# The subtraction of the state softmax's maximum moves from Pool to VectorE, right behind the transposes of the scores

## The chip, the core and the metric

The kernel runs on one core of a Trainium2 chip. The metric is the time of one execution on the device, in microseconds (us). The core has five engines that run side by side, each through its own instructions in order: PE (TensorE, matmuls and transposes; weight loads are listed apart as PEld), DVE (VectorE), ACT (ScalarE), POOL (GpSimd) and SP (SyncE, which issues the DMAs). An instruction that depends on another engine's result waits on a semaphore, and everything behind it on its own engine waits too.

## The reference

Three stages follow each other. The first is a two-way attention between 512 tokens and 32 state rows per head, for 8 batches (b) of 8 heads with 64 columns each:

```python
scores = scale * np.matmul(x, state.transpose(0, 1, 3, 2))      # tokens x states
a = softmax(scores, axis=-1)                                    # over the 32 states
xread = np.matmul(a, state)
scores2 = scale * np.matmul(state, x.transpose(0, 1, 3, 2))     # states x tokens
scores2 = scores2 - scores2.max(-1, keepdims=True)              # over the 512 tokens
a2 = np.exp(scores2)
a2 /= a2.sum(-1, keepdims=True) + 1e-09
sread = np.matmul(a2, x)
```

The second is a soft mixture of experts over all 4608 rows (512 tokens and 32 state rows per batch) with 8 experts of 4 slots; the third is a gated unit, `(silu(x @ w_gate) * (x @ w_val)) @ w_out`, on the same rows. Everything is in float32, and the result is compared with the reference in float32.

## The kernel before

**Stages.** The attention loop handles one batch per turn, b = 0 to 6, and then batch 7 in a tail of its own that works in halves. After it come the slots of the mixture (up to about 106 us), the two groups of experts, whose weights stream in while they run (up to about 145 us), and a main loop of 17 blocks of rows times 6 pieces of the gated unit (from about 152 us to the end). The order of the instructions on every engine is the order of the calls in the source: it is written out by hand.

**One turn of the attention loop.** `scores(b)` multiplies the states by the tokens on PE (L241): rows are 4 heads x 32 states, two groups q = 0, 1, columns are 512 tokens. ACT copies the product with the scale into the buffer `stsA` (L250, named atA in the profile; there is one such buffer, used by all batches). `scores_max(b)` takes the negated maximum over the 512 tokens on DVE (L255, tile nm). These scores serve both softmaxes:

- `attn_sub(b)` transposes the *unshifted* scores on PE in 8 pieces (the helper `tr8`, L267), so that tokens become rows, and DVE takes the maximum over the 32 states and subtracts it, in two halves (L277, L278, L277, L278). `attn_exp` takes the exponential of each half on ACT (L284), `attn_norm` sums on DVE and multiplies by the reciprocal on POOL (L291 to L295).
- `state_shift(b)` adds the negated maximum over the tokens to the scores in place, once per group q. It can only begin when the transposes of `attn_sub` have read the unshifted scores. `state_tr(b)` then transposes the shifted scores, also with `tr8` (L267, so one line has both transposes), and ACT takes the exponential of the whole (L311, tile e). The product with the tokens follows in the next turn (`sread_mm`, L321), and its division on DVE (L330 to L337).

Between these lie pieces of the batches b-1 and b-2: the transposes of the normalized weights (L344) and the products for the mixture's logits and slots (L354, L375, L382, L389, with ACT copies at L346, L363, L380 and L393). `load_T` (L233, L234) transposes the tokens of a later batch on PE, and ACT copies them. At b = 0 the projection of the states on the router stands in addition (L1005, with an ACT copy L1007).

**What sets the order around the change.** In the loop PE has: scores, transposes of a later batch, `sread_mm(b-1)`, logits of b-2, `attn_sub`'s 8 transposes, `attn_tr(b-1)`, `slots_mm(b-2)`, `state_tr`'s 8 transposes, `logits_mm(b-1)`. ACT has: the copy of the scores (L250), the copies of later tokens (L234), `logits_exp(b-2)`, two small copies, the two exponentials of `attn_exp` (L284), the exponential of `state_tr` (L311), two small copies (L363, L393), and the next turn's L250. The large PSUM tiles come from `pbig`, three buffers in turn, so the scores of the next turn take the buffer that `attn_sub`'s DVE instructions have read.

**The tail.** For batch 7 the maximum over tokens and `state_shift` follow both halves of L1030 and L1031 on DVE; then come `logits_tr(5)` (DVE copy L382), `slots_mm(5)` on PE between two rows of filler matmuls (L305), the halves' normalization (L1047 to L1052, one half of it on POOL), and `state_tr(7)`.

**The loads.** One SP queue issues all loads in order (L156) into a ring of 17 buffers; a load waits until its buffer is released by the matmuls that read it, or, for some expert weights, until an attention buffer is free (`free(...)`).

Of the kernel before, what the change touches and what calls it, by code (L numbers as in the profile page):

```python
# [12 lines left out]
ALU = mybir.AluOpType  # L13
# [47 lines left out]
def bc(ap, n):  # L61
    shape = list(ap.shape)
    return ap.rearrange("p (a o) -> p a o", o=1).to_broadcast([shape[0], shape[1], n])
# [3 lines left out]
def attn_moe_glu_kernel(  # L67
# [14 lines left out]
    pe, act, dve, pool = nc.tensor, nc.scalar, nc.vector, nc.gpsimd  # L82
# [43 lines left out]
    def pbig(shape, dt=F32):  # L126
        bcnt[0] += 1
        return psum(bcnt[0] % 3, shape, dt)
# [115 lines left out]
    def scores(b):  # L244
        x_ = xT.pop(b) if b in XT_PE else got.pop(("xt", b))
        p = pbig([128, 2, S])
        score_mm(b, x_, p, slice(0, S))
        done()
        t = stsA
        act.activation(out=t, in_=p, func=AF.Copy, scale=SCALE)  # L250
        sts[b] = t

    def scores_max(b):
        nm = sm.tile([128, 2], F32, tag="nm2", name="nm2")
        dve.tensor_reduce(out=nm, in_=sts[b], axis=AX.X, op=ALU.max, negate=True)  # L255
        RZ[b] = nm

    def state_shift(b):
        nm, t = RZ.pop(b), sts[b]
        for q in range(2):  # L260
            pool.tensor_scalar(out=t[:, q, :], in0=t[:, q, :], scalar1=nm[:, q:q + 1], scalar2=None, op0=ALU.add)  # L261

    def tr8(src):
        p = pbig([128, 4, 256])
        for j in range(4):
            for q in range(2):
                pe.transpose(p[:, j, q * 128:(q + 1) * 128], src[q][:, j * 128:(j + 1) * 128], ident)  # L267
        return p

    def attn_sub(b):  # L270
        t = sts[b]
        v = tr8([t[:, 0, :], t[:, 1, :]])
        a = wk.tile([128, 4, 256], F32, tag=f"a{b % 3}", name="a")
        for i in range(2):
            vi, ai = (u[:, 2 * i:2 * i + 2, :].rearrange("p j (h s) -> p (j h) s", s=NS) for u in (v, a))
            m1 = sm.tile([128, 16], F32, tag="m1", name="m1")
            dve.tensor_reduce(out=m1, in_=vi, axis=AX.X, op=ALU.max)  # L277
            dve.tensor_tensor(out=ai, in0=vi, in1=bc(m1, NS), op=ALU.subtract)  # L278
        A[b] = a

    def attn_exp(b):
        a = A[b]
        for i in range(2):
            act.activation(out=a[:, 2 * i:2 * i + 2, :], in_=a[:, 2 * i:2 * i + 2, :], func=AF.Exp)  # L284
# [12 lines left out]
    def heat(n, i=None, src=None):  # L297
        src = ident if src is None else src
        p = pbig([128, 128]) if i is None else psum(i, [128, 128])
        for _ in range(n):  # L300
            pe.matmul(out=p, lhsT=src, rhs=src, start=True, stop=True)
# [5 lines left out]
    def state_tr(b):  # L307
        t = sts[b]
        p = tr8([t[:, 0, :], t[:, 1, :]])
        e = wk.tile([128, 4, 256], F32, tag="e2", name="e2")  # L310
        act.activation(out=e, in_=p, func=AF.Exp)  # L311
        E2N[b] = e

    def sread_mm(b):
        x_, e = got.pop(("xn", b)), E2N.pop(b)
        p = psmall([128, 130])
        for q in range(2):
            for j in range(4):
                for c in range(4):
                    k = 128 * q + 32 * c  # L320
                    pe.matmul(out=p[32 * c:32 * c + 32, 65 * q:65 * q + 65], lhsT=e[:, j, k:k + 32],  # L321
                              rhs=x_[:, j, c, 65 * q:65 * q + 65],
                              start=(j == 0), stop=(j == 3))
        done()
        P4[b] = p

    def sread_out(b):
        p = P4.pop(b)
        z = sm.tile([128, 2], F32, tag="z2", name="z2")
        dve.tensor_scalar(out=z, in0=p[:, 0:130:129], scalar1=EPS, scalar2=None, op0=ALU.add)  # L330
        r2 = sm.tile([128, 2], F32, tag="r2", name="r2")
        dve.reciprocal(out=r2, in_=z)
        o = 32 * (b % 4)
        for c in range(4):
            dst = srC[o:o + 32, b // 4, 2 * c:2 * c + 2, :]
            cc = slice(32 * c, 32 * c + 32)
            dve.tensor_tensor(out=dst, in0=p[cc, 1:129].rearrange("p (q d) -> p q d", q=2), in1=bc(r2, D)[cc], op=ALU.mult)  # L337

    def attn_tr(b):
        a = A[b]  # L340
        p = pbig([128, 2, S])
        for j in range(4):
            for q in range(2):
                pe.transpose(p[:, q, j * 128:(j + 1) * 128], a[:, j, q * 128:(q + 1) * 128], ident)  # L344
        t = wk.tile([128, 2, S], F32, tag="at", bufs=1, name="at")
        act.copy(out=t, in_=p)  # L346
        AT[b] = t

    def logits_mm(b):
        t = AT.pop(b)  # L350
        p = psmall([128, 128])
        for q in range(2):
            for j in range(4):
                pe.matmul(  # L354
                    out=p[32 * j:32 * j + 32, :], lhsT=SP[:, b, q, :], rhs=t[:, q, j * 128:(j + 1) * 128],
                    start=(q == 0), stop=(q == 1),
                )
        P6[b] = p
# [8 lines left out]
    def logits_exp(b, n=128):  # L367
        t = LE[b]
        act.activation(out=t[:n, 1, :], in_=t[:n, 0, :], func=AF.Exp, bias=md[:n, b:b + 1], accum_out=ds[:n, b:b + 1])

    def logits_tr(b):
        t = LE.pop(b)
        p = psmall([128, 2, 128])
        for i in range(2):
            pe.transpose(p[:, i, :], t[:, i, :], ident)  # L375
        e = wk.tile([128, 128], F32, tag="edn", bufs=2, name="edn")
        lg = Lg[:, 2 + 4 * b:6 + 4 * b, :]
        for f in (1, 0) if b == B - 3 else (0, 1):
            if f:
                act.copy(out=lg, in_=p[:, 0, :].rearrange("p (j s) -> p j s", s=NSL))  # L380
            else:
                dve.tensor_copy(out=e, in_=p[:, 1, :])  # L382
        EdN[b] = e

    def slots_mm(b, alloc=psmall):
        e, a = EdN.pop(b), A.pop(b)
        p = alloc([128, 256])
        for j in range(4):
            pe.matmul(out=p[32 * j:32 * j + 32, :], lhsT=e[:, 32 * j:32 * j + 32], rhs=a[:, j, :], start=True, stop=True)  # L389
        P4["q"] = p  # L390
# [4 lines left out]
    def build_stB(g):  # L395
        p = psum(g, [128, 4, 128])
        for pr in range(4):
            pe.transpose(p[:, pr, :], stN[:, g, 2 * pr:2 * pr + 2, :].rearrange("p h d -> p (h d)"), ident)
        dve.tensor_copy(out=stB[:, 4 * g:4 * g + 4, :, :], in_=p.rearrange("p r (b s) -> p b r s", s=NS))
# [550 lines left out]
    with tc.manual_schedule():  # L950
# [16 lines left out]
        def ok(b):  # L967
            return 0 <= b < B

        def at(b, k):  # L970
            for half in range(2):
                if k in (LT[half], 99):
                    load_T(b + 1, half)

        at(-1, 99)
        for b in range(B - 1):
            scores(b)
            at(b, 0)
            if ok(b - 2):
                logits_exp(b - 2)  # L980
            scores_max(b)
            if b == 0:
                heat(HB)
                build_stB(1)
            if ok(b - 1):
                sread_mm(b - 1)
                sread_out(b - 1)
            if ok(b - 2):
                logits_tr(b - 2)
            attn_sub(b)  # L990
            state_shift(b)
            if ok(b - 1):
                attn_tr(b - 1)
            attn_exp(b)
            if ok(b - 2):
                slots_mm(b - 2)
            state_tr(b)
            attn_norm(b)
            if b == 0:
                p = pbig([128, 2, 512])  # L1000
                for bb in range(B):
                    for pr in range(4):
                        for hh in range(2):
                            r = slice(64 * hh, 64 * hh + 64)
                            pe.matmul(out=p[32 * pr:32 * pr + 32, hh, 32 * bb:32 * bb + 32], lhsT=stB[r, bb, pr, :],  # L1005
                                      rhs=phs[r, pr, :], start=True, stop=True)
                act.copy(out=SP.rearrange("p b q s -> p q b s"), in_=p[:, :, 0:256].rearrange("p q (b s) -> p q b s", s=NSL))  # L1007
            if ok(b - 1):
                logits_mm(b - 1)
                logits_max(b - 1)  # L1010
            if ok(b - 2):
                slots_out(b - 2)
            if b == 5:
                sr_T(0)
            if b == 6:
                sr_mm(0)

        b = B - 1
        x_ = xT.pop(b) if b in XT_PE else got.pop(("xt", b))
        t = stsA  # L1020
# [374 lines left out]
```

## Time and profile before

| quantity | value |
|---|---|
| median of 3 runs | 490.19 us (488.57, 490.19, 491.98) |
| profiled execution | 489.67 us, of which 487.6 us from the first to the last instruction |
| mean granted TensorE clock | 0.993 of full speed |
| PE busy | 452.9 us (93%) |
| DVE busy | 314.4 us (64%) |
| ACT busy | 254.7 us (52%) |
| POOL busy | 181.9 us (37%), of which L261 24.9 us in 16 instructions |
| moved by DMA | 74.36 MB |

The span is the stretch from the first to the last instruction of the profiled execution; the run's own time has 2.07 us around it. Busy time counts only instructions that compute. In the timeline, a row gives the start, the length, the engine, the line of the source, the operation, the tiles out<-in with their shapes, how many instructions were merged, and in square brackets the idle time of the engine just before, with what ended it. Ends of matmuls are modelled, and the records of neighbouring instructions of one engine can overlap by about a tenth of a microsecond.

### The profile page before, as it was taken

Reading aid. Unit: us, or ns where it says so; the run is one execution under the profiler, and the core shown is the slowest. Engines: PE = TensorE matmul, PEld = TensorE weight load, DVE = VectorE, ACT = ScalarE, POOL = GpSimd, SP = SyncE. Lnnn points to the kernel's source line nnn. Section 1 sums busy time; section 2 is a strip of 40 time slices with the busy share of each in tenths; the row PEclk is TensorE's granted clock in tenths of the full one; section 3 lists DMA queues with packets and bytes.
Section 4 is the critical chain, followed back from the end, with each engine's and each line's share of the span. In section 5 each row is a group of like instructions: output and inputs, shape, how many; then the busy total and the mean of one; then the engine's idle time right before and its main releaser. Section 6 shows DMA issues by size and latency. Waiting matters only on the chain.

```text
span 487.6 us, 9247 instructions
## 1 busy us (share of the span) xinstructions
PE 452.9 (93%) x3661; PEld 248.5 (51%) x3661; DVE 314.4 (64%) x627; ACT 254.7 (52%) x432; POOL 181.9 (37%) x150
## 2 busy tenths in 40 slices
PE   7788888899898998998999899899999999999996
PEld 5555566654445454454455354455555555555553
DVE  3577767856928966868989879876433344344454
ACT  1366776433616988777456365545444444444441
POOL 1354444308203433343343243342433333333331
PEclk9799999999999999999999999999999999999999
DMA  8999992869999940102000000000011112112124
GB/s 310 425 417 414 416 382 66 309 228 379 419 400 422 417 171 2 57 30 86 2 1 1 0 1 0 1 1 3 0 44 43 44 43 69 61 46 76 54 86 172
DMA packets 16218, 74.36 MB, mean 152 GB/s; under 512 B 1584, under 2 KB 2992, under 8 KB 9392
## 3 DMA queue, kind: packets, MB, share of 16 engines
q1 hardware_dynamic: 16176, 73.78, 38.6%
q8 instruction: 28, 0.46, 0.4%
q14 instruction: 14, 0.11, 0.1%
HBM read 64.87 MB, written 8.91 MB: 151 GB/s over the span
## 4 chain that ended last, share of the span: by engine, by line
PE 75%; DVE 9%; DMA 4%; issue 4%; POOL 3%; ACT 3%; SPq 0%; ACTq 0%; DVEq 0%; POOLq 0%
PE p L1279 49%; PE p L1245 8%; DMA u<-in_wo_dram 3%; POOL atA L261 3%; PE p L267 3%; PE p L241 2%; PE p L481 2%; PE p L512 1%; DVE sh L1250 1%; DVE gvf L567 1%; PE s L321 1%; PE s L732 1%; PE p L233 1%; DMA u<-in_xt_dram 1%; PE s L744 1%
## 5 line engine op out<-in xcount | busy, mean ns | idle before, releaser
L1279 PE MATMUL p<-wo,hl 128*128 128x512 f16 x1020 | 235.1, 379 | 4.4 <-DVE osb L1290 3.3
L1259 POOL TENSOR_TENSOR hl<-sh,hl 128x512 f16<-128x512 f32 x102 | 125.9, 1235 | 202.3 <-ACT hl L1258 111.6
L1279 PEld LDWEIGHTS <-hl 128*128 128x128 f16 x1224 | 119.1, 98 | 130.0 <-issue 4.7
L1250 DVE SCALAR_TENSOR_TENSOR sh<-p,segk,sh 128x512 f32<-128x512 f32 x102 | 76.4, 749 | 93.8 <-ACT sh L1246 85.7
L1258 ACT CAST hl<-sh 128x512 f16<-128x512 f32 x102 | 62.9, 617 | 115.9 <-PE p L1279 80.9
L1246 ACT ACTIVATE sh<-p,sg 128x512 f32<-128x512 f32 x85 | 58.4, 686 | 5.7 <-PE p L1245 1.0
L1290 DVE SCALAR_TENSOR_TENSOR osb<-p,segm,osb 128x512 f32<-128x512 f32 x62 | 45.3, 746 | 10.9 <-PE p L1279 10.9
L1279 PE MATMUL p<-bqm,hl 128*128 128x512 f16 x204 | 46.8, 379 | 0.0
L1245 PE MATMUL p<-cstack,gvs 128*128 128x256 f16 x272 | 41.2, 273 | 2.7 <-DVE gvs L778 1.4
L261 POOL TENSOR_SCALAR atA<-atA,nm 128x512 f32<-128x512 f32 x16 | 24.9, 1566 | 38.3 <-PE p L267 23.3
L1245 PEld LDWEIGHTS <-gvs 128*128 128x128 f16 x272 | 25.9, 98 | 20.9 <-issue 3.2
L267 PE MATMUL p<-cs,atA 128*128 128x128 f32 x120 | 19.4, 298 | 12.5 <-POOL atA L261 10.8
L267 PEld LDWEIGHTS p<-cs,atA 128*128 128x128 f32 x120 | 14.6, 150 | 17.0 <-POOL atA L261 16.9
L1245 PE MATMUL p<-cstack,gv 128*128 128x256 f16 x136 | 20.6, 273 | 0.9 <-DVE segm L805 0.9
L255 DVE TENSOR_REDUCE nm<-atA 128x2 f32<-128x1024 f32 x8 | 9.7, 1219 | 14.3 <-ACT atA L250 14.3
L1288 ACT ACTIVATE osb<-p,segk 128x512 f32<-128x512 f32 x26 | 17.1, 687 | 3.3 <-PE p L1279 3.1
L567 DVE SCALAR_TENSOR_TENSOR gvf<-u,gvf 128x512 uint32<-128x512 uint32 (+1 forms) x22 | 18.6, 860 | 0.1
L295 POOL TENSOR_TENSOR a<-a,r 128x1024 f32<-128x1024 f32 x7 | 13.4, 1916 | 13.8 <-DVE r L294 13.8
L571 DVE SCALAR_TENSOR_TENSOR gvf<-u,gvf 128x512 uint32<-128x512 uint32 (+1 forms) x22 | 18.1, 846 | 0.1
L1245 PEld LDWEIGHTS <-gv 128*128 128x128 f16 x136 | 13.0, 98 | 10.1 <-issue 1.7
L512 PE MATMUL p<-u,exq 128*32 128x256 f32 x256 | 14.8, 381 | 1.5 <-DMA u<-in_w_dram 0.8
L561 ACT ACTIVATE gvf<-u 128x512 f32<-128x512 f32 (+1 forms) x22 | 15.3, 715 | 0.0
(254 smaller groups left out, 502.6 us busy)
## 6 DMA issues: line engine op xcount, KB each, us to landing
u<-in_w_dram SPq DMA_DIRECT2D x24, 1024.0 KB, 14.2
u<-in_wgv_dram SPq DMA_DIRECT2D x12, 1024.0 KB, 16.3
u<-in_xn_dram SPq DMA_DIRECT2D x8, 1040.0 KB, 18.1
out_dram<-osb SPq DMA_DIRECT2D x15, 512.0 KB, 2.8
early<-in_w_dram SPq DMA_DIRECT2D x12, 512.0 KB, 8.7
u<-in_wo_dram SPq DMA_DIRECT2D x5, 1024.0 KB, 13.9
u<-in_xt_dram SPq DMA_DIRECT2D x3, 1024.0 KB, 7.6
u<-in_wo_dram SPq DMA_DIRECT2D x2, 512.0 KB, 10.2
```

The costliest lines, as they stand in the source:

```text
L261: pool.tensor_scalar(out=t[:, q, :], in0=t[:, q, :], scalar1=nm[:, q:q + 1], scalar2=None, op0=ALU.add)
L267: pe.transpose(p[:, j, q * 128:(q + 1) * 128], src[q][:, j * 128:(j + 1) * 128], ident)
L512: pe.matmul(out=SO[g][i][32 * j:32 * j + 32, :], lhsT=hT[g, k // 4][:, k % 4, 32 * j:32 * j + 32], rhs=u[:, j, :], start=(k == 0), stop=(k ...
L567: dve.scalar_tensor_tensor(out=tu[:, c], in0=lo[:, c], scalar=29, in1=tu[:, c], op0=ALU.logical_shift_right, op1=ALU.bitwise_or)
L571: dve.scalar_tensor_tensor(out=tu[:, c], in0=hi[:, c], scalar=0x80000000, in1=tu[:, c], op0=ALU.bitwise_and, op1=ALU.bitwise_or)
L1245: pe.matmul(out=p[v][:, 256 * i:256 * i + 256], lhsT=GV[2 * q + i][v], rhs=rhs, start=True, stop=True)
L1246: act.activation(out=sh[:, 0, :], in_=p[0], func=AF.Silu, scale=sgs[q])
L1250: dve.scalar_tensor_tensor(out=sh[:, 1, :], in0=p[1], scalar=(kap0[0] if k == 0 else seg_scale(*seg)[0][q]), in1=sh[:, 0, :], op0=ALU.mult ...
L1258: act.copy(out=t[:, 0, :], in_=sh[:, 1, :])
L1259: pool.tensor_tensor(out=t[:, 1, :], in0=sh[:, 1, :], in1=t[:, 0, :], op=ALU.subtract)
L1279: pe.matmul(out=accs[i], lhsT=t[:, u // 2, c], rhs=WO[2 * q + j][:, u % 2, :], start=first and u == 0 and j == 0, stop=last and (j, u) == ...
L1290: dve.scalar_tensor_tensor(out=o, in0=a, scalar=rsc, in1=o, op0=ALU.mult, op1=ALU.add)
```

## The change

Both calls of `state_shift` now issue their two instructions on DVE instead of POOL. In the loop the call also moves: from behind `attn_sub(b)` into it, directly behind the 8 transposes, and so ahead of the DVE maxima and subtractions of the other softmax. In the tail the call stays where it was (behind `scores_max`), on the other engine. Nothing else changes; no DMA is issued by these lines.

```diff
     def state_shift(b):
         nm, t = RZ.pop(b), sts[b]
         for q in range(2):
-            pool.tensor_scalar(out=t[:, q, :], in0=t[:, q, :], scalar1=nm[:, q:q + 1], scalar2=None, op0=ALU.add)
+            dve.tensor_scalar(out=t[:, q, :], in0=t[:, q, :], scalar1=nm[:, q:q + 1], scalar2=None, op0=ALU.add)
...
     def attn_sub(b):
         t = sts[b]
         v = tr8([t[:, 0, :], t[:, 1, :]])
+        state_shift(b)
         a = wk.tile([128, 4, 256], F32, tag=f"a{b % 3}", name="a")
...
             attn_sub(b)
-            state_shift(b)
             if ok(b - 1):
                 attn_tr(b - 1)
```

## Rows read from the trace of the kernel before

**Rows 1.** Waits of PE: waited for, us in total, times, longest us.
```profile
PE p L267 <- POOL atA L261: 10.8, 14, 1.2
```

**Rows 2.** Timeline, one steady turn (b = 4 into b = 5).
```profile
59.17 1.02 ACT L311 ACTIVATE e<-p 128x1024 f32<-128x1024 f32 x1 [0.63 <-PE p L267]
...
60.09 0.26 ACT L363 COPY le<-s 128x128 f32<-128x128 f32 x1
...
60.91 1.03 ACT L250 ACTIVATE atA<-p 128x1024 f32<-128x1024 f32 x1 [0.29 <-PE p L241]
...
64.38 1.04 PE L267 MATMUL p<-cs,atA 128*128 128x128 f32 x8
...
65.41 3.10 POOL L261 TENSOR_SCALAR atA<-atA,nm 128x512 f32<-128x512 f32 x2 [3.41 <-DVE srC L337]
65.55 0.68 DVE L277 TENSOR_REDUCE m<-p 128x16 f32<-128x512 f32 x1
...
68.31 0.63 ACT L284 ACTIVATE a<-a 128x512 f32<-128x512 f32 x1 [0.45 <-DVE a L278]
...
68.56 0.99 PE L267 MATMUL p<-cs,atA 128*128 128x128 f32 x7 [1.21 <-POOL atA L261]
...
69.59 1.02 ACT L311 ACTIVATE e<-p 128x1024 f32<-128x1024 f32 x1 [0.65 <-PE p L267]
```

**Rows 3.** Groups by line and shape, DVE: xcount | busy us, mean ns | idle.
```profile
L564 DVE TENSOR_SCALAR wof<-wof 128x512 uint32<-128x512 uint32 x11 | 4.6, 425 | 5.4 <-ACT wof L561 4.9
L491 DVE TENSOR_SCALAR exq<-p,rd 128x512 f32<-128x512 f32 x2 | 1.5, 751 | 3.3 <-PE p L481 3.3
```

**Rows 4.** Timeline, the first two turns (b = 0 and b = 1).
```profile
13.12 0.69 DVE L278 TENSOR_TENSOR a<-p,m 128x512 f32<-128x512 f32 x1
...
15.69 1.55 PE L1005 MATMUL p<-phs,atA 64*32 64x32 f32 x128
...
17.28 0.59 ACT L1007 COPY SP<-p 128x512 f32<-128x512 f32 x1 [0.46 <-PE p L1005]
...
18.58 1.02 ACT L250 ACTIVATE atA<-p 128x1024 f32<-128x1024 f32 x1 [0.71 <-PE p L241]
...
20.47 1.49 PE L321 MATMUL s<-u,e 128*32 128x65 f32 x62 [1.85 <-issue]
...
21.89 1.97 PE L267 MATMUL p<-cs,atA 128*128 128x128 f32 x8
...
22.39 1.18 DVE L337 TENSOR_TENSOR srC<-s,r 32x128 f32<-32x128 f32 x4
...
23.90 0.69 DVE L277 TENSOR_REDUCE m<-p 128x16 f32<-128x512 f32 x1 [0.32 <-PE p L267]
...
29.67 1.03 ACT L250 ACTIVATE atA<-p 128x1024 f32<-128x1024 f32 x1 [0.50 <-PE p L241]
```

**Rows 5.** DMA queues, 17.90 to 18.00 us: packets, MB, share of 16 engines.
```profile
q8 instruction: 1, 0.02, 57.8%
```

**Rows 6.** Windows: busy us (instructions) by engine, then PEclk, DMA share, GB/s.
```profile
22.00:23.00 1.00, 1.00 (x5) 1.00 (x6) 0.90 (x5) 0.00 (x0) 0.00 (x0) 0.50 0.99 416
```

**Rows 7.** Timeline, the tail of batch 7.
```profile
87.89 0.28 DVE L382 COPY edn<-s 128x128 f32<-128x128 f32 x1
...
88.15 3.11 POOL L261 TENSOR_SCALAR atA<-atA,nm 128x512 f32<-128x512 f32 x2 [4.74 <-DVE nm L255]
...
88.80 1.16 PE L305 MATMUL p<-cs 128*128 128x128 f32 x8
...
91.31 0.98 PE L267 MATMUL p<-cs,atA 128*128 128x128 f32 x7 [1.21 <-POOL atA L261]
```

**Rows 8.** Windows of 4 us, columns as in rows 6.
```profile
80.00:84.00 4.00, 3.59 (x67) 2.55 (x65) 1.77 (x5) 2.92 (x7) 1.91 (x1) 1.00 0.00 0
...
104.00:108.00 4.00, 4.00 (x71) 2.50 (x74) 2.54 (x8) 0.28 (x2) 0.00 (x0) 1.00 0.10 40
```

**Rows 9.** Chain that ended last, the experts: start us, us, what.
```profile
128.58 16.42 DMA u<-in_wo_dram
```

## The prediction

> **What bounds the kernel now.** I read the sum of PE's waits first: 14 times in the attention PE stands still for the subtraction on POOL, 10.8 us in all [rows 1]. That is the most that a reader could hope for, and it is not the gain, because another wait may stand close behind each of them. So I read one steady turn in the timeline [rows 2]. The transposes of the unshifted scores end at 65.42, the two subtractions on POOL take 3.10 us, PE idles 1.21 us before the last seven transposes of the shifted scores, these end at 69.55, and ACT's exponential L311 follows at 69.59. This is the chain now. The reader is to see its neighbour: ACT has just finished the second exponential L284 of the *other* softmax, at 68.94, which had waited for the DVE subtraction L278. The exponential L311 stands behind it in ACT's order. So the chain through DVE and ACT is only 0.65 us shorter than the one through POOL, and the change lengthens it, since the shift now stands ahead of L277 on DVE.
>
> **The price of the subtraction on DVE.** No row has a DVE `tensor_scalar` from SBUF to SBUF in float32 with a pointer scalar and 512 columns. The nearest is L564, in place, SBUF, 512 columns of 4 bytes, with an immediate: 0.425 us [rows 3]. That is the lower bound. L491 reads PSUM with a pointer scalar: 0.751 us [rows 3], the upper bound. I take 0.49: L564 shares memory, shape and in-place writing, and to it I add the 0.06 by which L491 lies above the 0.69 of L278, which also reads PSUM but has no pointer scalar [rows 3, 4]. Two independent neighbours overlap by about 0.08, so the pair delays DVE by 2 x 0.41 = **0.82 us** (bounds 0.69 and 1.34). [...]
>
> **The steady turn, step by step** [rows 2]. Call the start of L250 R and the start of L311 T.
> - T to the next R: L250 started at 60.91 after 0.29 idle, so ACT was free at 60.62; records overlap by 0.10 (L311 ends at 60.19, L363 starts at 60.09). From 59.17 that is 1.35 us. The wait for PE that cost 0.29 goes: PE gets to the next scores earlier.
> - R to the end of `attn_sub`'s transposes: 65.42 - 60.91 = 4.51. This is work of ACT and PE that the change leaves alone.
> - The shift on DVE: 0.82. POOL started at 65.41, DVE's L277 at 65.55, so DVE is free in time.
> - L277 to the second L284: 68.31 - 65.55 = 2.76, moved as a block.
> - L284 to L311 on ACT: 0.63 - 0.10 = 0.53.
>
> The sum is 9.97 us against 69.59 - 59.17 = 10.42. So a turn gains **0.45 us**, not the 1.2 that PE waits. The transposes of the shifted scores are no longer late: the shift is done by 66.3, PE reaches them at about 67.0 (68.56 less 1.21 and less the first of the eight) and ends by 68.1, while ACT is busy till about 69.8. What is late next is ACT's exponential, behind DVE. There are five such turns (from the R of b = 2 to that of b = 7): 2.25 us. Break-even is a pair of 1.27 us; at the upper bound a turn loses 0.07.
>
> **The first two turns** [rows 4]. At b = 0 the second L278 ended at 13.81; 0.82 later that is 14.63, L284 takes it to 15.2, then L311 (1.02), L1007 (0.59), less two overlaps: L250 of b = 1 at 16.6 instead of 18.58. L1005 does not hold this back: POOL's 3.10 becomes 0.90 ahead of it, and PE's transposes have less of a pause before them, so it starts some 2.5 us earlier, at 13.2, and ends by 14.8. Then comes a pause that no engine explains: L321 stops for 1.85 us and goes on at 20.47. A block of instructions moves at 17.90 in the middle of a saturated stream of loads [rows 5]. I read the pause as PE waiting for its next instructions, asked for at some point during L1005, so that the end of the pause moves with L1005: 20.47 - 2.5 = 18.0. PE's clock decides the rest. [...] Slow again, L321 ends at 19.5, the transposes at 21.4. At full clock the division on DVE, which ended 1.6 after L321, is the later one, at 20.7. The shift starts there, and 0.82 + 2.76 + 0.53 + 1.08 later (the last being L311 and L363 less overlaps) comes L250 of b = 2: at 25.9 to 26.6 instead of 29.67. That is 3.1 to 3.8; I take **3.4**.
>
> **The tail** [rows 7]. Here the shift stands ahead of the copy L382, which PE's next product and fillers wait for. L382 starts at 88.85 instead of 87.89; the fillers end 0.96 later than 89.96, at 90.92; eight transposes of 1.04 end at 91.96, before at 92.29: a gain of **0.33**. The half that POOL normalizes had stood behind POOL's shift and now waits for DVE instead, about as long.
>
> **What follows.** Only if the loads allow it does the rest move along. In the experts PE waits 16.42 us for a load [rows 9]; a stream bound by bandwidth would swallow the gain. But the stream had stood idle between: nothing at 80 to 84 us, 0.10 at 104 to 108 [rows 8], because loads wait for buffers that the attention and the first expert release. These releases move, so the landing moves. The main loop keeps its order and its load. On POOL and SP nothing is queued that wanted POOL earlier; no DMA is issued by the moved lines.
>
> **The sum.** 3.4 + 5 x 0.45 + 0.33 = 6.0 us off the profiled execution's 489.67 (span 487.6, 2.07 around it), which lies 0.5 below the median; off the median of 490.19 this is **484.2**. The pair's price counts eight times (two turns, five turns, the tail): at 0.69 each gain grows, in all by 1.0, to 483.2, with full clock 482.8; at 1.34 all shrink, by 4.2, to 488.4.
>
> **Rivals.**
> - *The pause stays where it is* (goes on at 20.47, whatever PE did before). For: no row names its releaser, and one packet is thin evidence. Then the shift of b = 1 begins at 23.90 as the maximum did, L250 of b = 2 comes at 29.1, 0.6 earlier instead of 3.4: 3.2 us in all, **487.0**. Against: the pause begins three matmuls after 128 quick ones, and the packet moved shortly before its end. [...] Chance 0.20.
> - *The pair costs the upper bound*, 1.34: the turns gain nothing, the first two 2.4, the tail loses 0.2: **488.4**. For it speaks the pointer scalar, against it L564. Chance 0.10.
> - *The loads swallow it*: the experts end with the same landing as before, **490.2**. Chance 0.08.
> - *Slower: DVE becomes the bound of each turn.* Everything in a turn is behind the shift on DVE: four maxima and subtractions, two exponentials, L311, and with it the next L250. With the pause moving, the kernel as a whole loses from a pair of 0.82 + 6.0/8 = 1.57 on, 0.83 per instruction; with the pause fixed (seven places, 3.2 us) from 1.28, 0.72 each. At 1.0 each, a pair of 1.84, it is **492.3**. For: it is a queue with no slack, 0.65 us from the chain today. Against: no 512-column row read here reaches 0.83. Chance 0.06.
>
> That the subtraction stays on POOL can't be; two lines decide it.
>
> **Chances and range.** The forecast has 0.56. About 1%, 4.9 us, is what a measurement of this kernel can tell from no change: below 485.3 is faster. The forecast's own range, 482.8 to 485.3, lies there for the most part, the rivals beside it: faster 0.52, same 0.44, slower 0.04. The range of 8 in 10 goes from 482.3 to 488.5; it takes in the fixed pause and the upper price, and leaves out the swallowed gain and the slower case.
>
> **What would show it.** Right: L261 on DVE at 0.42 to 0.55 us each; L311 released by ACT's own L284 (DVE L278) instead of PE; 9.9 to 10.1 us from one L250 to the next; L250 of b = 2 at 25.9 to 26.6; the load of rows 9 landing about 6 us earlier. Wrong: 0.7 us or more for L261, a pause of L321 that still ends at 20.4, transposes of the shifted scores that still release L311, or a landing that stays at 145.0.

## The result and the profile after

The changed kernel takes 485.48 us (median of 4 runs, 483.81 to 486.57), the kernel before, run beside it, 491.09 us: a ratio of 0.9891 (95% interval 0.9841 to 0.9940), 1.1% faster. The interval lies wholly below 1, so the gain is clear of the spread of the runs. The forecast was 484.2 us against 490.19, a ratio of 0.988, or 6.0 us less; measured are 5.6 us less. The profiled execution takes 485.54 us with a span of 483.8; POOL's busy time falls from 181.9 to 157.6 us, DVE's rises from 314.4 to 318.2. In the changed file the lines behind 273 stand one lower: L277, L278, L284, L311 and L321 of before are L278, L279, L285, L312 and L322.

**The price.** The group of the moved subtraction in the DVE table of the changed kernel (count, busy us, mean ns of one, idle before it); it answers to [rows 3]:

```profile
L261 DVE TENSOR_SCALAR atA<-atA,nm 128x512 f32<-128x512 f32 x16 | 7.0, 483 | 0.7 <-PE p L267 0.5
```

0.483 us each where 0.49 was taken; on POOL a pair took 3.10 [rows 2].

**A steady turn.** Timeline of the changed kernel, the turn that answers to [rows 2]:

```profile
56.58 1.01 ACT L312 ACTIVATE e<-p 128x1024 f32<-128x1024 f32 x1
...
57.49 0.26 ACT L364 COPY le<-s 128x128 f32<-128x128 f32 x1
...
57.90 1.05 ACT L250 ACTIVATE atA<-p 128x1024 f32<-128x1024 f32 x1
...
61.37 1.04 PE L267 MATMUL p<-cs,atA 128*128 128x128 f32 x8
...
62.33 0.88 DVE L261 TENSOR_SCALAR atA<-atA,nm 128x512 f32<-128x512 f32 x2 [0.17 <-PE p L267]
...
63.13 0.68 DVE L278 TENSOR_REDUCE m<-p 128x16 f32<-128x512 f32 x1
...
63.77 1.09 PE L267 MATMUL p<-cs,atA 128*128 128x128 f32 x8
...
65.90 0.63 ACT L285 ACTIVATE a<-a 128x512 f32<-128x512 f32 x1 [0.64 <-DVE a L279]
...
66.43 1.01 ACT L312 ACTIVATE e<-p 128x1024 f32<-128x1024 f32 x1
```

From one L312 to the next the turn takes 9.85 us (before 10.42). L312 has no bracket: it follows directly on ACT's own exponential, and that one waited 0.64 us for DVE. The transposes of the shifted scores are over at 64.86, 1.6 us before they are used. The waits of PE in the whole execution (us in total, times, longest) answer to [rows 1]:

```profile
PE s L376 <- ACT le L370: 3.4, 5, 0.7
...
PE p L241 <- DVE a L279: 1.8, 3, 0.6
...
PE p L267 <- DVE atA L261: 1.0, 2, 0.7
```

The 10.8 us of waiting for the shift are down to 1.0, yet the kernel gained only 5.6 us: PE now waits for ACT and DVE at other places.

**The first two turns,** timeline, answering to [rows 4]:

```profile
14.77 1.29 PE L1005 MATMUL p<-phs,atA 64*32 64x32 f32 x128
...
18.38 1.04 ACT L250 ACTIVATE atA<-p 128x1024 f32<-128x1024 f32 x1
...
20.25 1.10 PE L322 MATMUL s<-u,e 128*32 128x65 f32 x61 [1.88 <-issue]
...
23.01 0.88 DVE L261 TENSOR_SCALAR atA<-atA,nm 128x512 f32<-128x512 f32 x2
...
28.28 1.04 ACT L250 ACTIVATE atA<-p 128x1024 f32<-128x1024 f32 x1
```

A window of the changed kernel behind the pause (busy us and instructions of PE, PEld, DVE, ACT and POOL, then granted clock, DMA share, GB/s):

```profile
20.00:24.00 4.00, 3.38 (x79) 2.86 (x79) 3.10 (x10) 0.71 (x1) 0.49 (x1) 1.00 1.03 430
```

The granted clock is 1.00 here, where the kernel before had 0.50 [rows 6].

The start times of the first two turns look hardly earlier, and the reason has nothing to do with the change: the first load of tokens landed later (PE waited 2.58 us for it, before 0.83), so the first scores began at 8.95 us instead of 7.11. Stages are therefore counted from the first scores on. The table has the kernel before, the profiled execution of the changed kernel, and a second one (a0 below) whose first scores began at 7.04:

| stage, from the start of ... to the start of ... | before | predicted change | change, first profile | change, a0 |
|---|---|---|---|---|
| first scores to L250 of b = 1 | 11.47 | -1.97 | -2.04 | -2.01 |
| to L250 of b = 2 | 11.09 | -1.43 | -1.19 | -1.28 |
| to the scores' first copy of b = 7 (L1070) | 53.10 | -2.25 | -3.15 | -3.11 |
| to the first matmul of the experts | 23.23 | -0.33 | -0.18 | -0.18 |
| to the second group of the main loop's L1245 | 46.13 | 0 | +0.64 | +0.64 |
| to the end of the span | 335.50 | 0 | +0.20 | +0.81 |
| sum | 480.52 | -6.0 | -5.72 | -5.13 |

The attention, its tail included, gives 6.6 us, more than forecast; 0.8 to 1.5 us are given back behind it.

**The tail,** timeline, answering to [rows 7]:

```profile
83.46 0.88 DVE L261 TENSOR_SCALAR atA<-atA,nm 128x512 f32<-128x512 f32 x2
84.26 0.28 DVE L383 COPY edn<-s 128x128 f32<-128x128 f32 x1
...
86.16 1.04 PE L267 MATMUL p<-cs,atA 128*128 128x128 f32 x8
...
86.43 0.69 DVE L1052 TENSOR_TENSOR a<-a,r 128x512 f32<-128x512 f32 x1
86.56 1.46 POOL L1052 TENSOR_TENSOR a<-a,r 128x512 f32<-128x512 f32 x1 [6.24 <-DVE r L1050]
...
88.08 1.09 PE L1058 MATMUL p<-cs,a 128*128 128x128 f32 x8 [0.31 <-POOL a L1052]
```

The transposes end at 87.20, 8.97 us after L1070 (9.52 before), a gain of 0.55 us, but L1058 then waits for POOL's half of the normalization, which takes 1.46 us instead of 1.05.

**The experts.** The end of a gap in which PE waits for ACT's copy, and a window (columns as above) shortly after it, in the changed kernel and then in the kernel before:

```profile
123.14 1.08 PE L531 MATMUL s<-cs,so 128*128 128x32 f32 x8 [1.29 <-ACT so L529]
...
125.00:126.00 1.00, 1.00 (x12) 0.32 (x8) 0.97 (x3) 0.99 (x2) 0.00 (x0) 0.50 0.98 410
```

```profile
127.84 1.08 PE L530 MATMUL s<-cs,so 128*128 128x32 f32 x8 [1.28 <-ACT so L528]
...
129.00:130.00 1.00, 1.00 (x12) 0.27 (x9) 1.00 (x2) 0.98 (x2) 0.00 (x0) 1.00 0.98 410
```

After the same gap of 1.3 us the granted clock is 0.50 in one and 1.00 in the other. The load of [rows 9] is issued at 123.89 in the changed kernel and lands 16.3 us later, at 140.2, which is 6.6 us earlier than before when both are counted from the first scores.

### The profile page after: what moved, and what is told of

The parts are those of the page before. It is cut to its first block, busy times and chain, and to the rows that moved or that the text cites. A ratio compares the mean times of both kernels' runs of the same rounds, so it can differ in the third digit from the quotient of the medians.

```text
span 483.8 us, 9235 instructions
## 1 busy us (share of the span) xinstructions
PE 450.9 (93%) x3661; PEld 246.9 (51%) x3661; DVE 318.2 (66%) x643; ACT 253.1 (52%) x432; POOL 157.6 (33%) x134
## 3 DMA queue, kind: packets, MB, share of 16 engines
q1 hardware_dynamic: 16176, 73.78, 38.9%
## 4 chain that ended last, share of the span: by engine, by line
PE 71%; DVE 15%; ACT 8%; issue 3%; DMA 1%; POOL 0%; SPq 0%; DVEq 0%; ACTq 0%; POOLq 0%
PE p L1279 49%; PE p L1245 8%; PE p L482 3%; PE p L513 3%; DVE a L279 2%; ACT xT L234 2%; DVE m L278 2%; DMA u<-in_xt_dram 1%; DVE atA L261 1%; DVE sh L1250 1%; DVE gvf L568 1%; PE s L733 1%; ACT e L312 1%; PE s L745 1%; PE p L267 1%
## 5 line engine op out<-in xcount | busy, mean ns | idle before, releaser
L1279 PE MATMUL p<-bqm,hl 128*128 128x512 f16 x204 | 46.8, 379 | 0.0
L1245 PE MATMUL p<-cstack,gvs 128*128 128x256 f16 x272 | 41.2, 273 | 2.4 <-DVE gvs L891 1.3
L1245 PEld LDWEIGHTS <-gvs 128*128 128x128 f16 x272 | 25.9, 98 | 20.5 <-issue 3.2
L1245 PE MATMUL p<-cstack,gv 128*128 128x256 f16 x136 | 20.6, 273 | 0.9 <-DVE segm L806 0.9
L1245 PEld LDWEIGHTS <-gv 128*128 128x128 f16 x136 | 13.0, 98 | 10.1 <-issue 1.7
L267 PE MATMUL p<-cs,atA 128*128 128x128 f32 x120 | 16.4, 277 | 1.2 <-DVE atA L261 1.0
L267 PEld LDWEIGHTS p<-cs,atA 128*128 128x128 f32 x120 | 13.3, 141 | 4.2 <-DVE atA L261 2.4
L513 PE MATMUL p<-u,exq 128*32 128x256 f32 x256 | 14.6, 380 | 0.7 <-ACT exq L503 0.7
L285 ACT ACTIVATE a<-a 128x512 f32<-128x512 f32 x14 | 8.8, 631 | 11.2 <-DVE a L279 11.2
```

What stands on the lines that cost most here:

```text
L513: pe.matmul(out=SO[g][i][32 * j:32 * j + 32, :], lhsT=hT[g, k // 4][:, k % 4, 32 * j:32 * j + 32], rhs=u[:, j, :], start=(k == 0), stop=(k ...
L1245: pe.matmul(out=p[v][:, 256 * i:256 * i + 256], lhsT=GV[2 * q + i][v], rhs=rhs, start=True, stop=True)
L1279: pe.matmul(out=accs[i], lhsT=t[:, u // 2, c], rhs=WO[2 * q + j][:, u % 2, :], start=first and u == 0 and j == 0, stop=last and (j, u) == ...
```

## Experiments

**a0, the changed kernel again,** as the measure for the group below. 

> The changed kernel itself, again, as the measure for the others of this group. Theory (the chain of a turn runs through VectorE and ScalarE, a turn takes 9.9 us): again some 5 to 6 us below the kernel before, 484 to 486 us. If the first token load decides the difference between executions, the first scores start anywhere from 7.1 to 9.0 us and the total moves with them by the same amount.

Measured: 484.62 us (482.23 to 487.07) against 489.4, ratio 0.9899 (0.9839 to 0.9959). The first scores began at 7.04, and the attention repeats to 0.1 us (table above). The main loop then started at 146.12 instead of 152.13, but at its entry the granted clock fell too, to 0.53 in this window:

```profile
148.00:150.00 2.00, 2.00 (x10) 1.22 (x10) 1.97 (x6) 0.97 (x2) 1.16 (x1) 0.53 1.03 426
```

So an early or late first load does not decide the total alone: the first scores came 1.9 us earlier in this profile than in the first, and its span is 1.3 us shorter.

**e1, the engine alone.** The shift runs on DVE, but behind the four operations of the other softmax, where it had been called (diff against the changed kernel).

```diff
         v = tr8([t[:, 0, :], t[:, 1, :]])
-        state_shift(b)
...
             attn_sub(b)
+            state_shift(b)
```

> The engine alone: the subtraction on VectorE, but at its old place in the order, behind the four maxima and subtractions of the other softmax. Theory (place and engine are both needed): the shift ends about 8.2 us after the start of L250, the transposes of the shifted scores follow and release L311 at 9.3, so a turn takes 10.5 to 10.7 us, more than the 10.42 of before; with two slower first turns the kernel takes 491 to 493 us. Rival (the cheaper instruction is what helps, wherever it stands): a turn of at most 10.1 us, 485 to 487 us.

Measured: 497.58 us, ratio 1.0165 (1.0126 to 1.0203), slower than the kernel before. Timeline of a turn, and a window of an earlier one:

```profile
53.59 1.03 ACT L250 ACTIVATE atA<-p 128x1024 f32<-128x1024 f32 x1 [0.26 <-ACT QS L393]
...
60.92 0.87 DVE L261 TENSOR_SCALAR atA<-atA,nm 128x512 f32<-128x512 f32 x2
...
61.46 1.38 PE L267 MATMUL p<-cs,atA 128*128 128x128 f32 x8 [1.89 <-DVE atA L261]
...
62.88 1.02 ACT L311 ACTIVATE e<-p 128x1024 f32<-128x1024 f32 x1 [1.20 <-PE p L267]
...
64.59 1.03 ACT L250 ACTIVATE atA<-p 128x1024 f32<-128x1024 f32 x1 [0.26 <-ACT QS L393]
```

```profile
40.00:42.00 2.00, 2.00 (x17) 0.34 (x18) 0.41 (x2) 0.80 (x3) 1.74 (x1) 0.50 1.03 426
```

The rival is out: the cheap instruction at the old place loses, because DVE serves both softmaxes in order and L311 now waits for PE 1.20 us. Up to L311 the theory holds to a hundredth: the shift ends 8.20 us and L311 starts 9.29 us after L250. But the next L250 comes 1.71 us after L311 instead of 1.35, so even this turn takes 11.0 us, and the theory was too mild. The turns from b = 2 and 3 take 12.0 and 11.6 us, those of b = 5 and 6 some 13. The expectation did not count the clock: it was granted at 0.50 in the window above and at 0.985 over the run (a0 0.991). The new place with the shift still on POOL was not run; on POOL the shift already started as the transposes ended, after 3.41 us of idling [rows 2], so an earlier call had little to gain there.

**e2, the price doubled.** Two more instructions of the same form follow the pair.

```diff
             dve.tensor_scalar(out=t[:, q, :], in0=t[:, q, :], scalar1=nm[:, q:q + 1], scalar2=None, op0=ALU.add)
+        for q in range(2):
+            dve.tensor_scalar(out=t[:, q, :], in0=t[:, q, :], scalar1=ones[:, 0:1], scalar2=None, op0=ALU.mult)
```

> The price doubled: behind the two subtractions two more VectorE instructions of the same form (a multiplication by 1.0 in place, with a pointer scalar). Theory (the pair stands on the chain in eight places): 0.80 us more in each, a turn of 10.7 us, 6.4 us in all, so 491 to 492.5 us, about level with the kernel before. Rival (the transposes of the shifted scores have 1.5 us to spare before ScalarE, so there is room for it): no change from the changed kernel, 485 us.

Measured: 491.29 us, ratio 1.0036 (1.0013 to 1.0058); 6.7 us above a0, against 6.4 expected. Timeline:

```profile
50.70 1.05 ACT L250 ACTIVATE atA<-p 128x1024 f32<-128x1024 f32 x1
...
55.14 0.88 DVE L261 TENSOR_SCALAR atA<-atA,nm 128x512 f32<-128x512 f32 x2 [0.16 <-PE p L269]
55.93 0.88 DVE L263 TENSOR_SCALAR atA<-atA,ones 128x512 f32<-128x512 f32 x2
...
61.34 1.05 ACT L250 ACTIVATE atA<-p 128x1024 f32<-128x1024 f32 x1
```

A turn takes 10.64 us, 0.79 more than with one pair, and the other four of the five turns lose 0.79 or 0.80 too: what is added at this place appears in full, and the rival is out. That the totals agree as well is in part luck. In this execution, the slowest of the ten, the turn of b = 1 and the tail lose 2.2 and 2.0 us against a0 instead of 0.8, and the clock was granted at 0.985 over the run (a0 0.991): behind the pause of b = 1 the last 62 matmuls of `sread_mm` (L324) took 1.95 us, where 61 took 1.10 at 1.00 in the first profile. The pause was longer too, 2.32 us against 1.88 there. The run stands for the slower rival: a pair of about 1.6 us loses the whole gain, and a little more, as the break-even of 1.57 said.

**e3, the pause.** Four more filler matmuls at the kernel's start (`HA, HB = 11, 5` instead of `7, 5`). 

> The changed kernel with four more filler matmuls of float32 at its very beginning (eight more matmul records, eight more weight loads). Theory (the pause of 1.8 us in TensorE at b = 1 is TensorE waiting for its next block of instructions, so it belongs to a place in the instruction stream): it comes eight matmul records earlier, no longer behind the third matmul of L322 but behind about the eleventh of the sixteen records of the scores L241 of b = 1, which then delays L250 of b = 1. Rival (it belongs to the data or to the time): it stays behind the first matmuls of L322, with the same length.

Measured in one run: 487.3 us. Timeline, PE at b = 1:

```profile
15.30 1.07 PE L241 MATMUL p<-u,atA 64*32 64x512 f32 x11 [0.49 <-PE p L1005]
19.08 1.22 PE L241 MATMUL p<-u,atA 64*32 64x512 f32 x5 [2.71 <-issue]
```

The pause sits behind the eleventh record of L241 instead of the third of L322: it belongs to a place in PE's instructions, not to data or time. It is also longer here, 2.71 us, and L250 of b = 1 waits for it. That PE waits there for its next instructions is argued from this place and from the packet of instructions that moves shortly before; no row names what released it.

**e4, the next wait.** The shifted scores' exponential goes between ACT's two others.

```diff
-            attn_exp(b)
+            attn_exp(b, 0)
             if ok(b - 2):
                 slots_mm(b - 2)
             state_tr(b)
+            attn_exp(b, 1)
```

> The changed kernel with one change of ScalarE's order: the exponential of the shifted scores (L311 of before) goes between the two exponentials of the other softmax, instead of behind both. Theory (ScalarE's exponential, released by VectorE, is what is late next, while the shifted scores are ready 1.5 us before they are used): the next L250 starts 0.7 us earlier, a turn takes 9.2 us, five to six turns give 3.5 to 4.2 us, 481 to 482 us. Rival (the turn is bound by VectorE's own work or by TensorE): no change, 485 us.

Measured: 483.42 us, ratio 0.9865 (0.9825 to 0.9905), 1.2 us below a0, not 3 to 4, and the runs of the two overlap (481.44 to 484.15 against 482.23 to 487.07). The trace is what shows a gain: a turn takes 9.72 instead of 9.85. Timeline:

```profile
52.12 0.63 ACT L284 ACTIVATE a<-a 128x512 f32<-128x512 f32 x1 [0.65 <-DVE a L279]
52.66 1.01 ACT L311 ACTIVATE e<-p 128x1024 f32<-128x1024 f32 x1
...
53.49 1.09 PE L241 MATMUL p<-xT,atA 64*32 64x512 f32 x16 [0.90 <-DVE a L279]
```

ACT's wait ahead of its second exponential is gone (one of 0.65 us ahead of the first is left), but another chain was 0.13 us behind it: the next scores (L241) need the PSUM buffer that DVE's last subtraction has read, and behind them on PE stand the transposes of later tokens and then `sread_mm`, whose division DVE must do ahead of the next shift. The expectation had looked at the start of L250 alone. In this execution the clock was granted at 1.00 on average, and the way from the experts' first matmul to the main loop took 45.98 us.

**e8, that chain too.** In addition to e4, `sread_mm` goes ahead of the transposes of later tokens, and the logits' exponential ahead of their copies.

```diff
             scores(b)
-            at(b, 0)
             if ok(b - 2):
                 logits_exp(b - 2)
             scores_max(b)
...
                 sread_mm(b - 1)
-                sread_out(b - 1)
+            at(b, 0)
+            if ok(b - 1):
+                sread_out(b - 1)
```

> The changed kernel with the exponential of the shifted scores between the two others, as in e4, and two more changes of order: the product sread_mm of b-1 goes ahead of the transposes of later tokens on TensorE, and the exponential of the logits of b-2 ahead of the copies of later tokens on ScalarE. Theory (in e4 the turn runs round TensorE and VectorE: scores, 1.97 us of transposes, sread_mm, the division, the shift, the four operations, and back by the buffer that the scores take): without the transposes in that loop the maximum over tokens leads to the division at once, a turn takes 9.0 to 9.3 us instead of 9.72, 480 to 481.5 us. Rival (another wait stands there already, as in e4): no change from e4, 483.4 us.

Measured: 480.76 us (478.66 to 482.94), ratio 0.9811 (0.9754 to 0.9868), the fastest of all. Timeline:

```profile
43.83 1.11 PE L321 MATMUL s<-u,e 128*32 128x65 f32 x64
43.91 1.02 ACT L250 ACTIVATE atA<-p 128x1024 f32<-128x1024 f32 x1
44.88 1.97 PE L233 MATMUL p<-cs,u 128*128 128x128 f32 x16
...
52.96 1.02 ACT L250 ACTIVATE atA<-p 128x1024 f32<-128x1024 f32 x1
```

A turn takes 9.05 us, as forecast. That these reorderings need the shift off POOL was not run; it is argued from [rows 2], where the transposes of the shifted scores end 0.6 us after the second exponential of the other softmax, so that L311 could not go ahead of it without waiting.

**e9, the clock in the experts.** Five filler matmuls where PE waits for ACT's copy. 

> The changed kernel with five filler matmuls where TensorE waits 1.3 us for ScalarE's copy between the two groups of experts. Theory (the part of the gain that is missing after the experts went to TensorE's clock, granted at 0.50 for about 3.5 us after that gap in the changed kernel and at 1.00 in the kernel before): with the gap filled the clock stays at 1.00 there, and the way from the first matmul of the experts (L482) to the main loop's second group of L1245 takes 46.1 us as before, not 46.8. Rival (the loads cost it): 46.8 us with the clock at 1.00.

Measured in one run: 483.94 us; the way from the experts' first matmul to the main loop takes 47.58 us, longer than both. Timeline of PE, then a window:

```profile
120.83 1.38 PE L306 MATMUL s<-cs 128*128 128x128 f32 x10 [0.18 <-ACT cstack L466]
...
137.77 0.64 PE L513 MATMUL p<-u,exq 128*32 128x256 f32 x8 [0.74 <-DMA u<-in_w_dram]
```

```profile
142.00:144.00 2.00, 2.00 (x12) 1.24 (x5) 1.19 (x7) 0.37 (x1) 0.13 (x1) 0.51 1.01 418
```

The clock did stay at 1.00 at the filled gap. PE was then early, waited for the last weights of the experts (0.74 us) as in the kernel before (0.85), and the clock fell later, to 0.64 in the window of 140 to 142 us and to 0.51 in that of 142 to 144. So the time that was expected failed: the loss moved rather than went. The two parts tell more than the whole. L513 ends 38.3 us after the experts' first matmul (138.41 and 100.09), as in the kernel before (L512, 38.4) and not 39.1 as in the changed kernel, so with the clock at 1.00 there this part loses nothing; the 1.5 us come behind it, where the granted clock is down to 0.51. The run shows beside it that the last weights come a fixed time after the experts begin: L513 goes on 37.7 us after their first matmul (100.09 here), L512 of before at 143.77, 37.8 after 106.00.

**e10, POOL's half of the tail.** DVE's half of L1052 goes behind the division, so that DVE reads PSUM while POOL works.

```diff
             for i in range(2):
+                if i == 1:
+                    sread_out(b - 1)
                 (pool, dve)[NRM[i]].tensor_tensor(out=avs[i], in0=avs[i], in1=bc(r[:, 16 * i:16 * i + 16], NS), op=ALU.mult)
...
         halves_norm()
-        sread_out(b - 1)
```

> The changed kernel with one change in the tail: VectorE's half of the normalization (L1052) goes behind the division L331 to L338, so that it no longer runs while GpSimd works on the other half. Theory (two engines on SBUF at once make GpSimd slower: 1.46 us in the changed kernel, where the two halves overlap, 1.05 before, where VectorE was reading PSUM): GpSimd's half takes 1.05 us again, and L1058 starts 0.3 us earlier. Rival (GpSimd's time has another cause): 1.46 us as before.

Measured in one run: 484.47 us. Timeline:

```profile
85.41 1.05 POOL L1054 TENSOR_TENSOR a<-a,r 128x512 f32<-128x512 f32 x1 [6.24 <-DVE z L331]
...
86.54 0.66 PE L1060 MATMUL p<-cs,a 128*128 128x128 f32 x4
...
87.55 0.63 PE L1060 MATMUL p<-cs,a 128*128 128x128 f32 x4 [0.35 <-DVE a L1054]
```

POOL is back at 1.05 us, against 1.46 in the first profile and in a0, where the two halves overlap, and the first half of the transposes starts 8.83 us after the tail's first transposes (77.71) instead of 9.21. The second half then waits for DVE's later half, so nothing is won.

## Why the prediction was right, point by point

- **The price** was right: 0.483 against 0.49, the pair 0.80 against 0.82. The choice to stay near L564 and add 0.06 for the pointer scalar is borne out. A `tensor_tensor` of this shape in SBUF took 0.69 us on DVE (L1052). The break-even of a pair of 1.57 us is 0.87 per instruction, not the 0.83 that the prediction gives (1.57/2 and the overlap of 0.08); nothing else hangs on it.
- **The chain of a turn** was right. L312 is released by ACT's L285 and this by DVE; e2 shows that what stands at the shift's place counts in full, and e1 that the engine without the place would have cost 8 us, a part of it, as an estimate from the mean granted clock (0.985, before 0.993), through the clock.
- **The size of the five turns** was too small: 3.1 us instead of 2.25. The turns from b = 2, 3 and 4 take 9.92, 9.85 and 9.85 instead of 9.97; two of the three lie just under the 9.9 to 10.1 that was named as a sign. Most of these 0.12 us is that the shift starts 4.43 us after L250 rather than 4.51. The bracket of its row says that it waited for PE's transposes alone: the division on DVE was done by then, since PE reaches `sread_mm` earlier, while POOL's start before is put down to that division [rows 2]. The last two turns, which carry extra work of the state rows, were counted like the others; they fell from 11.01 and 10.85 to 10.32 and 10.01.
- **The first two turns** gave 3.2 to 3.3 us of the 3.4, and two misses cancel in it. L1005 came 2.8 us earlier against the first scores, not 2.5, but the end of the pause moved by only 2.1, so the pause ended about 0.4 us later than forecast. On the other hand the granted clock was 1.00 behind it, where the prediction took the middle between the full clock and the lengths of [rows 4] (L321 1.49, the transposes 1.97 us, with the granted clock at 0.50 in [rows 6]); the first profile has 1.10 and 1.09 in their place. In e9, whose attention is the same, the 61 matmuls of L322 behind the pause took 1.95 us instead of 1.10, and the way from the end of the pause to L250 of b = 2 8.9 us instead of 8.0: this much of the gain hangs on the execution, by these lengths on its clock, and not on the shift. The pause moves with PE's instructions, as e3 settles. The rival of a fixed pause is refuted, although the pause of the first profile ends at 20.25, near the 20.4 that was named as a sign of wrong: with the first scores 1.9 us earlier, in a0, it ends at 18.27, and in e9, whose first scores begin at 7.14, at 18.14. Its length goes from 1.57 us (e9) to 2.71 (e3); no run shows what ends it.
- **The tail** gave 0.18 instead of 0.33. The transposes end 0.55 us earlier, more than forecast, and the rest is lost behind them. "About as long" was wrong for POOL's half: it now runs beside DVE's half, and e10 shows that this overlap takes it from 1.05 to 1.46 us.
- **The loads** let the gain through, though the row was read wrongly. The 16.42 us of [rows 9] are that load's way from issue to landing, not a wait of PE, which was busy for 15.54 of them and stood 0.85 us for another load, at 143.77. The sign itself came true: in the kernel before, the first profile and a0 the load lands 38.9 to 39.0 us after the experts' first matmul, so it moves with them, 6.6 us earlier against the first scores.
- **The clock behind the attention.** "The rest moves along" was not quite right. 0.64 us go in the experts, and the clock is what differs there: five executions whose granted clock falls to 0.50 behind the gap (both profiles of the changed kernel, e3, e8, e10) need 46.8 us for that way, and two that keep 1.00 (before, e4) 46.1 and 46.0. e9 agrees in the part in which its clock was at 1.00. At the main loop's entry a0 loses 0.8 us while the granted clock is 0.62 and 0.53 (146 to 148 and 148 to 150 us); e3 and e8 have the same fall there, to 0.50 and 0.52 in a window of 2 us, and the same time from there to the end to 0.1 us. The 0.2 us of the first profile have another cause, since its clock was at 1.00 there, and that stays open; the other executions with 1.00 at the entry (before, e4, e9, e10) spread from 334.5 to 335.5 us. Why the clock falls after a gap in one execution and not after the same gap in another stays open too.

The mechanism was right, and the nearness of the total is in part luck: 0.9 us too little in the turns and 0.8 to 1.5 too much behind them cancel for the most part, and the result lies within 1.3 us of the forecast. It lies 0.2 us above the line of 485.3 that the prediction drew for "faster", since the kernel before took 0.9 us more beside it than on record; by the ratio it lies below that line.

## What to carry to other kernels

When an engine's wait is removed, price the chain that runs second before pricing the wait: here PE's 1.2 us per turn were worth 0.5, because ACT's exponential, behind DVE, stood 0.65 us behind. An instruction that moves into an in-order queue ahead of other work costs its length to all of that work (in e2 the second pair made a turn 0.79 us longer), so compute the length at which the move breaks even, and keep the order in which two consumers of one engine are served as a choice of its own. After a gain, look for the next wait at once: three changes of order (e8) gave 3.9 us more (484.62 to 480.76), although the kernel before ran 1.0 us longer beside e8 than beside a0.

## What the runs showed of the hardware

- A DVE `tensor_scalar` in place in SBUF, 128x512 float32 with a pointer scalar, takes 0.483 us on average, and 0.40 us from start to start in a pair; a pair of the same on POOL took 3.10 us.
- POOL's 128x512 float32 multiplication took 1.46 us (first profile, a0) while DVE ran a multiplication on two SBUF tensors for 0.56 us of it, and 1.05 us beside DVE's division, which reads PSUM (before, e10).
- PE stopped at one place of its instructions behind 128 small matmuls, for 1.57 us (e9) to 2.71 us (e3). A packet of instructions began to move 2.3 to 2.6 us before PE went on (17.8 and 20.25 in the changed kernel, 15.9 and 18.27 in a0, 16.6 and 19.08 in e3).
- After the gap of 1.3 us in PE's work between the two groups of experts, the granted clock fell to 0.50 in five executions (first profile, a0, e3, e8, e10) and stayed at 1.00 in two (before, e4); the way from the experts' first matmul to the main loop took 46.8 us with the fall and 46.0 to 46.1 us without.
